# Loading q in 1 KB runs of four tokens, with rows un-permuted in the store, 64x64 state tiles, a new load order and a list-scheduled TensorE order

## The chip, the cores and the metric

The kernel runs on one core of one Trainium2 chip. The metric is the device time in microseconds of one launch. Fast runs of one kernel lie within 1.3% of each other. The profiles are single executions; their spans are about 2 us shorter than the timed runs. A "step" below is one block of 128 tokens of one batch entry (24 steps), a "chunk" is 512 tokens, that is four steps (6 chunks).

In profile lines PE is TensorE, PEld its weight loads, DVE is VectorE, ACT is ScalarE, POOL is GpSimd, SP is SyncE, which issues the loads. PEclk is the clock that TensorE was granted, in tenths of full speed; DMA is the mean busy share of the 16 DMA engines. A line number such as L335 is the line of the kernel's text that recorded the instruction; it differs between kernels.

## The reference, cut to what matters

Decaying linear attention over blocks of 64 tokens, then a feed-forward layer with a sine-squared activation:

```python
# q, k, v: (4, 8, 768, 64) float32; lam: (8,)
for b in range(nb):
    intra = einsum('bhic,bhjc->bhij', qb, kb) * Dmask        # lam ** (i - j), causal
    intra = einsum('bhij,bhjd->bhid', intra, vb)
    inter = einsum('bhid,bhde->bhie', qb * lam_pow, kv_state)
    out[:, :, sl] = intra + inter
    kv_state = lam_block * kv_state + einsum('bhsd,bhse->bhde', kb_dec, vb)
x = out.transpose(0, 2, 1, 3).reshape(3072, 512)
h = x @ w_in                                                  # 512 -> 2048
s = sin(alpha * h)
return (h + s * s / (alpha + 1e-9)) @ w_out                   # 2048 -> 512
```

## The kernel before

The kernel is a list of operations, each with an engine, an assumed duration and its dependencies. A small model orders the operations of all engines but TensorE; TensorE follows the order in which they were recorded. It works on blocks of 128 tokens: scale q and k by powers of lam, transpose them (on TensorE for steps 0 to 12, by DMA from step 13 on), S = scores of the eight heads, mask, then per step O (state times q, plus S times v) and Z (new state). Each of the eight heads has 64 columns; two heads share the 128 rows.

```python
def load_one(nme, s):                    # one DMA of 256 KB for each of k, q, v of a step
    a = src[b, :, n * BL:(n + 1) * BL, :].rearrange("h p d -> p h d")      # runs of 64 floats = 256 B
    rec_load(lambda e: e.dma_start(dst[r][:, :, :], a), [f"{nme}32.{r}"], f"{nme}{r}", 321000, ...)

# att_O: state part, then scores times v, then the new state
for jp in range(HP):                     # four 128x128 matmuls on a block-diagonal state
    e.matmul(dst[:, jp, :], Zs[(s - 1) % 2][:, jp, :], qkT[jq][:, jp, :], start=(jp == 0), stop=False, ...)
for jp in range(HP):
    for h in range(2):                   # eight matmuls of 128 rows, 64 columns
        last = e.matmul(dst[64*h:64*h+64, jp, :], v2[c][:, 2*jp+h, :], S_m[j][:, 4*h+jp, :], ...)
# ... Z: eight 128x64 matmuls, then two copies of the state out of PSUM, one for each half

# store of 128 tokens: 128 rows of 2 KB
rec("ACT", lambda e: e.dma_start(out[row0:row0 + 128, :], osb[o][:, :]), 0, ...)

# start: loads k0 q0 k1 q1 v0 k2 q2 v1 k3 q3 v2 v3; then per step s = 0..3
#   att_S(s); warm(2); att_T(s + 1); warm(1); att_O(s)      (warm: dummy matmuls)
# then chunk 0: 16 groups grp_A (x @ w_in), 16 groups grp_B (@ w_out) with attention steps 4 to 7 at
# hand-picked places; chunk 1's grp_A with steps 8 to 11; from there grp_B(c) and grp_A(c + 1) alternate
```

Of the kernel before, what the change touches and what calls it, by code (L numbers as in the profile page):

```python
# [28 lines left out]
class Program:  # L29
# [41 lines left out]
    def schedule(self, hop=0.12, rate=270e3, lag=1.7, receipt=1.0, issue=0.6, begin=0.75, depth=2):  # L71
# [15 lines left out]
        pe_at = 0  # L87
# [5 lines left out]
        def release(op):  # L93
            for u in op.users:
                left[u] -= 1
                same = u.eng == op.eng and op.slot is None
                ready_at[u] = max(ready_at[u], op.end + (0.0 if same and op.eng == "PE" else hop))
                if not left[u] and u.eng != "PE":
                    pend[u.eng].append(u)
# [5 lines left out]
        def transfer(t, i):  # L105
            _, op = (sw, hw)[i].pop(0)
            if i and len(hw) == depth - 1:
                free["SP"] = max(free["SP"], t)
            op.end = t + op.nbytes / rate + receipt
            release(op)  # L110
            return op.end - receipt

        n = len(self.ops)
        while len(order) < n:
            best = None
            for e in self.ENGINES:
                if e == "PE":
                    if pe_at >= len(pe_seq):
                        continue
                    op = pe_seq[pe_at]  # L120
                    if left[op]:
                        continue
                    cand = (max(free[e], ready_at[op]), op)
                else:
                    if not pend[e] or (e == "SP" and len(hw) >= depth):
                        continue
                    t0 = min(max(free[e], ready_at[o]) for o in pend[e])
                    op = min((o for o in pend[e] if max(free[e], ready_at[o]) <= t0 + 1e-9),
                             key=lambda o: (o.prio, o.idx))
                    cand = (t0, op)  # L130
# [8 lines left out]
            e = op.eng  # L139
            if e == "PE":  # L140
                pe_at += 1
            else:
                pend[e].remove(op)
            op.start = t
            order.append(op)
            for u in op.soft_users:
                left[u] -= 1
                ready_at[u] = max(ready_at[u], op.start)
                if not left[u] and u.eng != "PE":
                    pend[u.eng].append(u)  # L150
# [79 lines left out]
def bass_lightning_attn__then__act_snake_kernel(  # L230
# [23 lines left out]
    NQ = 3  # L254
    FIRST_DT = 13
# [4 lines left out]
    NO = 4  # L260

    es = contextlib.ExitStack()
    with es:
# [9 lines left out]
        q32 = ring("q32", RL, [128, H, D], F32)  # L273
# [3 lines left out]
        q2 = [t[:, 0, :, :] for t in qk2]  # L277
# [3 lines left out]
        S_m = ring("S_m", 2, [128, 8, 128], BF16)  # L281
        Zs = ring("Zs", 2, [128, HP, 128], BF16)
# [7 lines left out]
        mask = sb("mask", [128, 128], BF16)  # L290
# [3 lines left out]
        lam_bc = sb("lam_bc", [128, H], F32)  # L294
        E_i = sb("E_i", [128, NB, H], I32)
        E_f = sb("E_f", [128, NB, H], F32)
        lnlam = sb("lnlam", [128, H], F32)
        lnL = sb("lnL", [128, NB, H], F32)
        Lq = sb("Lq", [128, NB, H], F32)
# [26 lines left out]
        wblk, gate = [], {}  # L326
# [4 lines left out]
        def load_one(nme, s):  # L331
            src, dst = {"k": (k, k32), "q": (q, q32), "v": (v, v32)}[nme]
            b, n, r = s // NB, s % NB, s % RL
            a = src[b, :, n * BL:(n + 1) * BL, :].rearrange("h p d -> p h d")
            rec_load(lambda e: e.dma_start(dst[r][:, :, :], a), [f"{nme}32.{r}"], f"{nme}{r}", 321000,  # L335
                     [gate[s]] if s in gate else [])
# [6 lines left out]
        def consts():  # L343
            rec("ACT", lambda e: e.dma_start(lam_bc[:, :], bass.AP(lam.tensor, 0, [[0, 128], [1, H]])), 0,
                writes=["lam"], slot="lam", nbytes=4096)
            rec("ACT", lambda e: e.preload_act_table_set("natural_log_exp_and_others"), 1.3, writes=["table"])
            rec("POOL", lambda e: e.memset(zeros[:, :], 0.0), 0.5, writes=["zeros"])
            rec("POOL", lambda e: e.iota(E_i[:, :, :], [[128, NB], [0, H]], base=0, channel_multiplier=1), 0.2,
                writes=["E_i"])
            rec("DVE", lambda e: e.tensor_copy(E_f[:, :, :], E_i[:, :, :]), 0.2, reads=["E_i"], writes=["E_f"])  # L350
            rec("ACT", lambda e: e.activation(lnlam[:, :], lam_bc[:, :], ACTF.Ln), 0.3,
                reads=["lam", "table"], writes=["lnlam"])
            ln_b = bass.AP(lnlam, 0, [[H, 128], [0, NB], [1, H]])
            rec("DVE", lambda e: e.tensor_tensor(lnL[:, :, :], E_f[:, :, :], ln_b, ALU.mult), 0.2,
                reads=["E_f", "lnlam"], writes=["lnL"])
            rec("ACT", lambda e: e.activation(Lq[:, :, :], lnL[:, :, :], ACTF.Exp), 0.3,
                reads=["lnL"], writes=["Lq"])
            rec("ACT", lambda e: e.activation(Lk[:, :, :], lnL[:, :, :], ACTF.Exp, scale=-1.0), 0.3,
                reads=["lnL"], writes=["Lk"])
            rec("DVE", lambda e: e.memset(maskf[:, :], 0.0), 0.2, writes=["maskf"])  # L360
# [4 lines left out]
                out=mask[:, :], in_=maskf[:, :], pattern=[[-1, 128]], compare_op=ALU.is_gt, fill=1.0,  # L365
# [4 lines left out]
            for i in range(2):  # L370
                rec("DVE", lambda e, i=i: e.memset(Zs[i][:, :, :], 0.0), 0.3, writes=[f"Zs.{i}"])
# [15 lines left out]
        def w_block(j, soft=(), after=()):  # L387
            if j < 4:
                cs = slice(512 * j, 512 * (j + 1))
                src = moe_w_in[:, cs].rearrange("(c p) f -> p c f", p=128)  # L390
                op = rec("POOL", lambda e: e.dma_start(w1[:, :, cs], src), 0.85, writes=[f"w1.{j}"],
                    slot=f"w1_{j}", nbytes=723000, soft=soft, after=after)
            else:
                j2 = j - 4
                src = moe_w_out[512 * j2:512 * (j2 + 1), :].rearrange("(m p) d -> p m d", p=128)
                op = rec("POOL", lambda e: e.dma_start(w2[:, 4 * j2:4 * (j2 + 1), :], src), 0.85, writes=[f"w2.{j2}"],
                    slot=f"w2_{j2}", nbytes=723000, soft=soft, after=after)
            wblk.append(op)

        def prep(s, fast=False, soft=()):  # L400
            n, r, c = s % NB, s % RL, s % RC
            Lq_b = bass.AP(Lq, n * H, [[NB * H, 128], [1, H], [0, D]])
            Lk_b = bass.AP(Lk, n * H, [[NB * H, 128], [1, H], [0, D]])
            dve_k, dve_q = s == 3, fast and s != 2
            done = rec("DVE" if dve_k else "POOL", lambda e: e.tensor_tensor(k2[c], k32[r][:, :, :], Lk_b, ALU.mult),
                       0.65 if dve_k else 1.05, reads=[f"k32.{r}", "Lk"], writes=[f"k2.{c}"], soft=soft)
            rec("DVE" if dve_q else "POOL", lambda e: e.tensor_tensor(q2[c], q32[r][:, :, :], Lq_b, ALU.mult),
                0.65 if dve_q else 1.05, reads=[f"q32.{r}", "Lq"], writes=[f"q2.{c}"], soft=soft)
            if not soft:
                prep_v(s)  # L410
# [7 lines left out]
        def prep_v(s, soft=()):  # L418
            r, c = s % RL, s % RC
            rec("ACT", lambda e: e.copy(v2[c][:, :, :], v32[r][:, :, :]), 0.62,  # L420
                reads=[f"v32.{r}"], writes=[f"v2.{c}"], soft=soft)

        def att_T(s, bank=None):
# [8 lines left out]
            def pe(e):  # L432
                for jp in range(HP):
                    last = e.transpose(dst[:, jp, :], q2[c][:, 2 * jp:2 * jp + 2, :], ident[:, :])  # L434
# [3 lines left out]
            rec("PE", pe, 0.5, reads=[f"q2.{c}", f"k2.{c}", "ident"], writes=[key])  # L438
            rec("DVE", lambda e: e.tensor_copy(qkT[j][:, :, :], dst), 0.7, reads=[key], writes=[f"qkT.{j}"], prio=-1)  # L439

        def att_S(s):
            j, j2 = s % NQ, s % 2

            def pe(e):
                for jp in range(HP):
                    for h in range(2):
                        rows = slice(64 * h, 64 * h + 64)
                        last = e.matmul(A_ps[:, 4 * h + jp, :], qkT[j][rows, 4 + jp, :], qkT[j][rows, jp, :])  # L448
# [280 lines left out]
```

## Time and profile before

| | before |
|---|---|
| median of the timed runs | 225.18 us (224.98 to 225.64, 3 runs) |
| first feed-forward matmul (chunk 0, first half) | 23.04 us |
| second half of chunk 0 begins | 37.77 us |
| chunk 1 begins | 60.50 us |
| second half of chunk 1 begins | 81.48 us |
| TensorE ends / span ends | 220.20 / 222.92 us |

The milestones are start times of the first matmul of each group of feed-forward matmuls in the trace. From the page of the kernel before: busy time of the engines, then the span in 40 slices of 5.6 us (a digit is tenths), then the queue of the loads.

```profile
span 222.9 us, 3787 instructions
...
PE 209.1 (94%) x1513; PEld 102.9 (46%) x1539; DVE 119.7 (54%) x160; ACT 121.8 (55%) x216; POOL 133.9 (60%) x141
...
PE   6865999998999999999999999999999999999995
...
PEclk9999799999999999999999999999999999999999
DMA  6999999999999999999999533063031011100212
...
q1 hardware_dynamic: 86640, 21.90, 52.3%
...
PE 81%; DVE 6%; SPq 5%; DMA 3%; ACT 2%; issue 2%; POOL 0%
```

TensorE is busy nearly everywhere after the fourth slice. DMA reads 9 (90% or more) from slice 2 to slice 22, to some 120 us, and 6 or less after that. The last line, from the chain of work that ended last, puts 81% of the span on TensorE. So TensorE bounds the long second half, and loads bound the start.

The DMA issues of the same page, with count, size and median time from issue to landing:

```profile
out_dram<-osb ACTq DMA_DIRECT2D x23, 256.0 KB, 2.7
...
k_0<-in_k_dram SPq DMA_DIRECT2D x4, 256.0 KB, 5.1
q_0<-in_q_dram SPq DMA_DIRECT2D x4, 256.0 KB, 4.8
...
qkT<-qk_3 SPq DMA_TRANSPOSE x3, 3.2
```

### The profile page before, as it was taken

The page shows a single profiled execution, that of the slowest core. Times are in us where ns is not written, and L with a number is a line of the kernel's source. Part 1 is how long each engine was busy: PE and PEld are TensorE (multiplying, and loading weights), DVE is VectorE, ACT ScalarE, POOL GpSimd, SP SyncE. Part 2 cuts the span into 40 slices and gives each one's busy share as a digit, 9 for nine tenths or more (in the row PEclk, how much of TensorE's full clock was granted, in tenths as well). Part 3 has the DMA queues.
Part 4 walks back from the last instruction along what each step waited for, and adds up shares of the span by engine and source line. Part 5 has one row for each costly group of instructions (what it writes and reads, how often), then busy time and mean ns, then how long its engine had stood idle before and what let it go on. Part 6 is the DMA issues. An engine that isn't in the chain of part 4 may idle for free.

```text
span 222.9 us, 3787 instructions
## 1 busy us (share of the span) xinstructions
PE 209.1 (94%) x1513; PEld 102.9 (46%) x1539; DVE 119.7 (54%) x160; ACT 121.8 (55%) x216; POOL 133.9 (60%) x141
## 2 busy tenths in 40 slices
PE   6865999998999999999999999999999999999995
PEld 2443344454555444445445444445445444444454
DVE  2674189736868994645545454553553535544300
ACT  3354688131498976575575556566556435544220
POOL 3464378661389998668768867867845553355000
PEclk9999799999999999999999999999999999999999
DMA  6999999999999999999999533063031011100212
GB/s 133 219 216 201 195 196 220 162 229 229 268 284 221 222 201 236 215 244 180 245 221 201 141 94 94 1 96 96 19 79 47 0 50 47 47 37 10 79 65 94
DMA packets 94513, 32.50 MB, mean 146 GB/s; under 512 B 87184, under 2 KB 91552, under 8 KB 94496
## 3 DMA queue, kind: packets, MB, share of 16 engines
q1 hardware_dynamic: 86640, 21.90, 52.3%
q0 software_dynamic: 4224, 4.19, 11.4%
q10 hardware_dynamic: 3632, 6.17, 7.6%
q8 instruction: 12, 0.20, 0.4%
q14 instruction: 5, 0.04, 0.1%
HBM read 27.28 MB, written 6.29 MB: 151 GB/s over the span
## 4 chain that ended last, share of the span: by engine, by line
PE 81%; DVE 6%; SPq 5%; DMA 3%; ACT 2%; issue 2%; POOL 0%
PE m_ps L509 34%; PE m_ps L537 34%; SPq L335 5%; PE A_ps L473 3%; PE A_ps L448 3%; DMA v_3<-in_v_dram 3%; DVE gT L527 2%; PE A_ps L469 2%; PE m_ps L562 2%; DVE S_m L453 1%; PE A_ps L434 1%; PE Z_ps L488 1%; PE A_ps L436 1%; DVE u_3 L525 1%; DVE qkT L439 1%
## 5 line engine op out<-in xcount | busy, mean ns | idle before, releaser
L509 PE MATMUL m_ps<-xT,w 128*128 128x512 bf16 x366 | 92.5, 382 | 2.3 <-issue 1.7
L537 PE MATMUL m_ps<-w,gT 128*128 128x512 bf16 x362 | 90.6, 379 | 0.6 <-issue 0.3
L537 PEld LDWEIGHTS m_ps<-w,gT 128*128 128x128 bf16 x368 | 34.9, 98 | 42.2 <-ACT osb L549 1.3
L509 PEld LDWEIGHTS m_ps<-xT,w 128*128 128x128 bf16 x384 | 35.1, 98 | 41.3 <-issue 1.5
L453 DVE TENSOR_TENSOR S_m<-A_ps,mask 128x1024 bf16<-128x1024 f32 x24 | 29.4, 1223 | 9.7 <-PE A_ps L448 9.7
L525 POOL TENSOR_TENSOR u_0<-t_0 128x512 bf16<-128x512 bf16 x16 | 16.6, 1038 | 13.9 <-ACT t_0 L513 13.9
L527 DVE SCALAR_TENSOR_TENSOR gT<-u_3,r_sb,m_ps 128x512 bf16<-128x512 bf16 x16 | 11.9, 744 | 15.0 <-POOL u_3 L525 14.9
L482 ACT CAST xT<-A_ps 128x512 bf16<-128x512 f32 x20 | 11.7, 586 | 15.1 <-PE A_ps L473 15.0
L525 POOL TENSOR_TENSOR u_2<-t_2 128x512 bf16<-128x512 bf16 x15 | 15.6, 1037 | 7.3 <-ACT t_2 L513 7.3
L525 POOL TENSOR_TENSOR u_4<-t_4 128x512 bf16<-128x512 bf16 x15 | 15.6, 1039 | 7.0 <-ACT t_4 L513 7.0
L527 DVE SCALAR_TENSOR_TENSOR gT<-u_5,r_sb,m_ps 128x512 bf16<-128x512 bf16 x16 | 11.9, 746 | 14.1 <-POOL u_5 L525 14.1
L527 DVE SCALAR_TENSOR_TENSOR gT<-u_1,r_sb,m_ps 128x512 bf16<-128x512 bf16 x16 | 11.9, 744 | 14.0 <-POOL u_1 L525 14.0
L527 DVE SCALAR_TENSOR_TENSOR gT<-u_0,r_sb,m_ps 128x512 bf16<-128x512 bf16 x16 | 11.9, 743 | 11.5 <-POOL u_0 L525 11.5
L549 ACT COPY osb<-m_ps 128x512 f32<-128x512 f32 x19 | 11.1, 585 | 11.7 <-PE m_ps L537 11.7
L525 POOL TENSOR_TENSOR u_5<-t_5 128x512 bf16<-128x512 bf16 x12 | 12.5, 1039 | 7.9 <-ACT t_5 L513 7.8
L513 ACT ACTIVATE t_0<-m_ps,alpha_sb 128x512 bf16<-128x512 f32 x16 | 11.0, 685 | 10.8 <-PE m_ps L509 10.8
L513 ACT ACTIVATE t_2<-m_ps,alpha_sb 128x512 bf16<-128x512 f32 x16 | 11.0, 687 | 10.7 <-PE m_ps L509 10.5
L525 POOL TENSOR_TENSOR u_3<-t_3 128x512 bf16<-128x512 bf16 x12 | 12.5, 1038 | 7.3 <-ACT t_3 L513 7.2
L513 ACT ACTIVATE t_4<-m_ps,alpha_sb 128x512 bf16<-128x512 f32 x16 | 11.0, 687 | 10.7 <-PE m_ps L509 10.7
L525 POOL TENSOR_TENSOR u_1<-t_1 128x512 bf16<-128x512 bf16 x12 | 12.4, 1037 | 7.2 <-ACT t_1 L513 7.2
L496 ACT CAST Zs<-Z_ps 64x256 bf16<-64x256 f32 x40 | 14.6, 366 | 1.6 <-DVE qkT L439 1.0
L513 ACT ACTIVATE t_3<-m_ps,alpha_sb 128x512 bf16<-128x512 f32 x16 | 11.0, 687 | 8.0 <-PE m_ps L509 8.0
(190 smaller groups left out, 238.0 us busy)
## 6 DMA issues: line engine op xcount, KB each, us to landing
out_dram<-osb ACTq DMA_DIRECT2D x23, 256.0 KB, 2.7
w<-in_moe_w_in_dram POOLq DMA_DIRECT2D x4, 512.0 KB, 11.5
w<-in_moe_w_out_dram POOLq DMA_DIRECT2D x4, 512.0 KB, 12.8
k_0<-in_k_dram SPq DMA_DIRECT2D x4, 256.0 KB, 5.1
q_0<-in_q_dram SPq DMA_DIRECT2D x4, 256.0 KB, 4.8
k_1<-in_k_dram SPq DMA_DIRECT2D x4, 256.0 KB, 5.2
q_1<-in_q_dram SPq DMA_DIRECT2D x4, 256.0 KB, 5.6
v_0<-in_v_dram SPq DMA_DIRECT2D x4, 256.0 KB, 4.9
```

Source lines behind the costliest of these rows:

```text
L335: rec_load(lambda e: e.dma_start(dst[r][:, :, :], a), [f"{nme}32.{r}"], f"{nme}{r}", 321000, [gate[s]] if s in gate else [])
L448: last = e.matmul(A_ps[:, 4 * h + jp, :], qkT[j][rows, 4 + jp, :], qkT[j][rows, jp, :])
L453: rec("DVE", lambda e: e.tensor_tensor(S_m[j2][:, :, :], A_ps[:, :, :], mask_b, ALU.mult), 1.25, reads=["S0", "S1", "mask"], writes=[f"S_m ...
L473: last = e.matmul(dst[64 * h:64 * h + 64, jp, :], v2[c][:, 2 * jp + h, :], S_m[j][:, 4 * h + jp, :], start=(not has_state and jp == 0), st ...
L482: rec("ACT", lambda e: e.copy(xT[x][:, :, col:col + 128], dst), 0.6, reads=[key], writes=[f"x.{x}.{s % 4}"], prio=-1)
L496: rec("ACT", lambda e, rows=rows, cols=cols: e.copy(Zs[j][rows, :, cols], Z_ps[rows, :, :]), 0.4, reads=["Z"], writes=[f"Zs.{j}"])
L509: last = e.matmul(m_ps[i][:, :], w1[:, kc, 128 * m:128 * (m + 1)], xT[x][:, kc, :], start=(kc == 0), stop=(kc == NKC - 1))
L513: rec("ACT", lambda e: e.activation(t16[tt][:, :], m_ps[i][:, :], ACTF.Sin, scale=alpha_sb[:, m:m + 1]), 0.65, reads=[f"m.{i}", "alpha"], ...
L525: return e.tensor_tensor(u16[tt][:, :], t16[tt][:, :], t16[tt][:, :], ALU.mult)
L527: rec("DVE", lambda e: e.scalar_tensor_tensor(out=gT[g][:, m, :], in0=u16[tt][:, :], scalar=r_sb[:, m:m + 1], in1=m_ps[i][:, :], op0=ALU.m ...
L537: last = e.matmul(m_ps[bank][:, :], gT[g][:, m, 128 * s4:128 * (s4 + 1)], w2[:, m, :], start=(m == 0), stop=(m == NM - 1))
L549: rec("ACT", lambda e: e.copy(osb[o][:, :], m_ps[bank][:, :]), 0.6, reads=[f"m.{bank}"], writes=[f"o.{o}"])
```

## The change

Its intent: q in runs of 256 B costs the DMA engines more per byte than longer runs (in the trace a packet of 256 B takes 18 ns and one of 1 KB 46 ns), and loads bound the start. If a partition holds four neighbouring tokens of one head, a run is 1 KB. The tokens of a block then come out in another order (all with token mod 4 = 0 first, and so on), which the mask takes into account and the store undoes. Beside that, the state is kept as 64x64 tiles (one copy out of PSUM instead of two), k and q are loaded first and v last, the first w_in block is halved, and TensorE's order comes from list scheduling: of the next 40 recorded operations the model takes the one that is ready, with 0.2 us of slack for those recorded earlier.

The diff, cut to its core:

```diff
 # load
+            if nme == "q":
+                for h in range(2):
+                    a = src[b, h::2, n * BL:(n + 1) * BL, :].rearrange("g (p t) d -> g p (t d)", t=4)
+                    rec_load(lambda e, h=h, a=a: e.dma_start(
+                        q32[r][:, h, :, :].rearrange("p t d -> p (t d)"), a), [f"q32.{r}.{h}"], f"q{r}{h}", 112000)
 # store
-                rec("ACT", lambda e: e.dma_start(out[row0:row0 + 128, :], osb[o][:, :]), 0,
+                dst = out[row0:row0 + 128, :].rearrange("(p t) d -> t p d", t=4)
+                rec("ACT", lambda e: e.dma_start(dst, osb[o][:, :]), 0,
 # q columns of head pair jp, for S and for the state matmuls
+            return qkT[j][rows, 0:4, 32 * jp:32 * jp + 32]
 # state: 64x64 tiles, Z recorded before O
-                        e.matmul(dst[:, jp, :], Zs[(s - 1) % 2][:, jp, :], qkT[jq][:, jp, :], ...
+                        for h in range(2):
+                            rows = slice(64 * h, 64 * h + 64)
+                            e.matmul(dst[rows, jp, :]..., Zs[(s - 1) % 2][rows, jp, :], q_cols(jq, rows, jp), ...
 # TensorE order
-                    op = pe_seq[pe_at]
+                    ready = [o for o in ready if pe_rank[o] < pe_at + window]
+                op = min((o for o in ready if max(free[e], ready_at[o]) <= t0 + (slack if e == "PE" else 0) + 1e-9), ...
 # start
-        for what in ("k0", "q0", "k1", "q1", "v0", "k2", "q2", "v1", "k3", "q3", "v2", "v3"):
+        for what in ("k0", "q0", "k1", "q1", "k2", "q2", "k3", "q3", "v0", "v1", "v2", "v3"):
 # ... start: prep, transposes and scores of steps 0 to 3 first, then their output matmuls;
 # steps 4 to 7 recorded before grp_B of chunk 0, all their scalings released by chunk 0's last grp_A;
 # DMA transposes from step 12 on; more buffers for qkT and S_m (cut)
```

## The prediction

> **What bounds the kernel now.** The page gives TensorE 94% busy and 81% of the chain that ended last. Three phases:
>
> 1. Start-up, 0 to 23.0 us (timeline: first feed-forward matmul at 23.04 us), bound by the load queue: twelve q, k, v loads leave one per 1.18 us, the last (v of step 3) landing at 19.10 us. Then 3.9 us of chain: v copy, xT copy, two state copies (0.76 us), state and score matmuls at a granted clock of 0.66, xT copy.
> 2. First chunk, 23 to 60.5 us. DMA share is about 1.2; TensorE has 1.6 us of visible gaps between 40 and 58 us, the largest, 0.95 us, for q of step 7, landed at 53.27 us.
> 3. Steady state, 60.5 to 220 us, bound by TensorE alone. 512-column matmuls start every 216 ns. Each change between full and half-array shapes adds about 93 ns of spacing (149 instead of 56 ns between the last state matmul and the first S_m matmul).[...] A step costs about 0.43 us for S and 0.79 us for state, S_m and Z matmuls.
>
> **What the change does.**
>
> - q loads: 1024 packets of 256 B (18 ns median each) become 256 of 1 KB; 1 KB packets of the last stores took 46 ns. Estimate over 16 engines: 1.15 us becomes 0.74, so 0.4 us per step: 1.6 us by step 3, 3.3 us by step 7.[...]
> - v last, a first w1 block of half size, v copies spread over POOL, DVE and ACT, one state copy for two: v of step 3 lands near 17 us, the chain after it shrinks to 2 to 2.5 us. First feed-forward matmul: 19.3 us (18.3 to 20.5), a gain of 3.7 us, all critical.
> - First chunk: list scheduling and lighter loads remove 1 to 2 us of gaps. The second chunk's first group starts near 55.3 us instead of 60.5.
> - 64x64 state matmuls: four at 56 ns become four pairs at about 56 ns, no gain by themselves. Z first and the 64x64 shape add up to two shape changes per step with state: +0.19 us at worst[...]. I take +0.08 us over 13 such steps: +1 us, critical in the steady state.
> - One transposed step less on TensorE: -0.45 us.
> - Score, weight, tail and store work: unchanged (store packets stay 2 KB).
>
> Sum: -5.2 + 1.0 - 0.4 = -4.6 us.
>
> **Predicted time: 220.6 us, 217.5 to 223.8 in 8 of 10. Faster by over 2%: 0.50; within 2%: 0.47; slower by over 2%: 0.03.**
>
> **What would show it right or wrong.** Timeline: first feed-forward matmul near 19.3 us. DMA packets: 25,000 fewer of 256 B, 6,000 more of 1 KB, near 46 ns. Waits: 40 to 58 us loses the wait for q. Steady state: last 64x64 state matmul to first S_m matmul near 149 ns[...]; second chunk's start to the end 162.4 us before, 162 to 164 after.
>
> **What would make it wrong.** TensorE sits too idle before 19 us and starts at a low clock; w1 blocks land later than the earlier matmuls need them, giving the start-up gain back as waits; shape changes cost the full 0.19 us; the modelled TensorE order mispredicts landings and stalls; or, on the good side, the list schedule closes more gaps.

Four passages are cut where marked. -5.2 us at the start and in the first chunk (60.5 to 55.3), +1.0 for the changes of shape and -0.4 for one transposed step less give the -4.6 us.

## More of the kernel before

The longest waits of TensorE before (total us, times, longest):

```profile
PE m_ps L469 <- ACT Zs L496: 1.8, 1, 1.8
PE m_ps L579 <- POOL ident L361: 1.8, 1, 1.8
...
PE A_ps L434 <- DVE qk_2 L407: 1.0, 1, 1.0
```

No wait of the whole kernel is longer than 1.8 us.

## The result, and the profile after

The changed kernel takes 284.85 us (284.2 to 285.32, 4 runs) against 225.22 us before (with a fourth run); the ratio of the fast runs is 1.2643 (95% interval 1.2611 to 1.2675). Here and below a ratio is the mean time of one kernel's fast runs over that of the kernel before in the same rounds, so it isn't quite the ratio of the medians quoted. The change is 60 us slower where I had predicted 4.6 us faster.

From the page after:

```profile
span 282.4 us, 3953 instructions
...
PE 225.5 (80%) x1587; PEld 106.8 (38%) x1613; DVE 121.6 (43%) x158; ACT 117.7 (42%) x198; POOL 137.9 (49%) x147
...
PE   7447895899768687099939938967999999999990
...
PEclk9995699799997999689988997995999999999997
DMA  3469998797435568787586579695123111111122
...
q1 hardware_dynamic: 69060, 22.16, 39.5%
...
PE 56%; DMA 21%; SPq 11%; DVE 5%; issue 2%; ACT 1%; POOL 1%; POOLq 0%
```

TensorE's busy time grew from 209 to 225 us, but its share fell from 94% to 80%, and on the chain that ended last DMA went from 3% to 21%, the SP queue from 5% to 11%. The DMA row reads 5 to 8 through most of slices 5 to 28, where before it read 9: loads still hold the kernel back, and for longer, but with fewer DMA engines busy: the mean share of these slices is 0.75, where it was 1.15 in slices 2 to 22 before (the share can read above 1).

The milestones of the two traces (start of the first feed-forward matmul of each group), in us:

| | before | after | stretch up to this row longer by |
|---|---|---|---|
| v of step 3 landed | 19.10 | 27.18 | |
| chunk 0 first half begins | 23.04 | 30.53 | 7.5 (start) |
| chunk 0 second half begins | 37.77 | 50.77 | 5.5 |
| chunk 1 begins | 60.50 | 75.95 | 2.5 |
| chunk 1 second half begins | 81.48 | 105.36 | 8.4 |
| TensorE ends | 220.20 | 275.75 | 31.7 |
| span ends | 222.92 | 282.39 | 3.9 (tail) |

More than half of the loss lies behind the point from which I had called the kernel bound by TensorE alone. TensorE waits there for transposes that go by DMA, 22.3 us in all. The longest waits of TensorE after (total us, times, longest):

```profile
PE A_ps L480 <- DMA qkT<-qk_2: 13.4, 2, 7.8
PE A_ps L480 <- DMA qkT<-qk_0: 4.6, 1, 4.6
PE m_ps L577 <- DVE gT L567: 4.6, 1, 4.6
```

The DMA issues of the kernel after:

```profile
out_dram<-osb ACTq DMA_DIRECT2D x23, 256.0 KB
...
k_0<-in_k_dram SPq DMA_DIRECT2D x4, 256.0 KB, 7.6
q_0<-in_q_dram SPq DMA_DIRECT2D x8, 128.0 KB
...
qkT<-qk_2 SPq DMA_TRANSPOSE x3, 8.1
```

Two things stand out. The same k load that took 5.1 us from issue to landing takes 7.6 us, and transposes that took 3.2 to 3.8 us before take 4.8 to 8.1 us. And the two kinds of DMA whose shape was changed, the loads of q and the stores, have lost their landing time altogether. The SP queue shows how long each issue of a load held it at the start. Before (start us, us, engine, line, operation):

```profile
5.71 1.14 SPq L335 DMA_DIRECT2D k_2<-in_k_dram  x1
6.90 1.14 SPq L335 DMA_DIRECT2D q_2<-in_q_dram  x1
8.09 1.13 SPq L335 DMA_DIRECT2D v_1<-in_v_dram  x1
```

After:

```profile
8.31 1.05 SPq L345 DMA_DIRECT2D k_2<-in_k_dram  x1
9.41 2.60 SPq L341 DMA_DIRECT2D q_2<-in_q_dram  x2
12.05 1.33 SPq L345 DMA_DIRECT2D k_3<-in_k_dram  x1
13.43 2.76 SPq L341 DMA_DIRECT2D q_3<-in_q_dram  x2
```

One tile of q holds the queue for 2.6 us, where it held it for 1.14 us. I had estimated 0.74 us.

The packets, counted by size on the load queue, say why. They add up to the page's totals (86,640 and 69,060):

```
load queue          256 B     1 KB    4 B
before             84,992      128   1,520
after              61,440    6,272   1,348
```

The packets of 1 KB have a median of 46 ns and those of 256 B 18 ns, both as predicted. The last column is the key. The number of 4-byte packets is a fixed one for each DMA, and the counts agree exactly: before, 72 loads x 16 + 11 transposes x 32 + 1 half store x 16 = 1,520. After, 48 loads of k and v x 16 + 12 transposes x 32 + 48 loads of q x **4** + 1 half store x **4** = 1,348. The source of a q load, `"g (p t) d -> g p (t d)"`, has the four head pairs as its slowest dimension, where the loads with 16 have 128 tokens. The store, `"(p t) d -> t p d"`, has the 4 of the token order as its slowest dimension; on its queue the 4-byte packets went from 416 (26 DMAs x 16) to 132 (25 x 4 + 2 x 16).

The same number shows in how many packets are under way at a time, counted from their start times and durations in the two traces. Of the time that any is under way, the 1 KB packets of the load queue after are most often four at a time (41%; 7 at most), and so are the 2 KB packets of the stores (57%; 7 at most). Before, the 2 KB packets of the stores are most often 16 at a time (22%; 20 at most). So I read the number of 4-byte packets of a load or a store as the number of DMA engines that work on it, and say "on 4 engines" for it; the traces don't name the engine of a packet. In this case's profiles every issue group on fewer than 16 engines in this sense lacks its landing time. That is what the missing numbers meant.

An estimate from these durations fits: a k tile is 1024 packets of 18 ns on 16 engines, 1.15 us; a q tile is 2 DMAs of 128 packets of 46 ns on 4 engines, 2 x 32 x 46 ns = 2.94 us. Together 4.1 us for each pair of k and q; in the trace k of steps 1, 2 and 3 lands at 10.32, 14.25 and 18.13 us, 3.9 us apart. Before, one load landed every 1.18 us.

### The profile page after: what moved, and what is told of

Read it like the earlier page. It is cut to its first block, busy times and chain, and to the rows that moved or that the text cites. A ratio compares the mean times of both kernels' runs of the same rounds, so it can differ in the third digit from the quotient of the medians.

```text
span 282.4 us, 3953 instructions
## 1 busy us (share of the span) xinstructions
PE 225.5 (80%) x1587; PEld 106.8 (38%) x1613; DVE 121.6 (43%) x158; ACT 117.7 (42%) x198; POOL 137.9 (49%) x147
## 3 DMA queue, kind: packets, MB, share of 16 engines
q1 hardware_dynamic: 69060, 22.16, 39.5%
## 4 chain that ended last, share of the span: by engine, by line
PE 56%; DMA 21%; SPq 11%; DVE 5%; issue 2%; ACT 1%; POOL 1%; POOLq 0%
PE m_ps L577 24%; PE m_ps L549 24%; SPq L341 8%; DMA qkT<-qk_2 6%; SPq L345 4%; DMA qkT<-qk_0 3%; DMA w<-in_moe_w_out_dram 3%; DMA qkT<-qk_4 3%; DMA q_5<-in_q_dram 2%; PE A_ps L480 2%; DMA v_3<-in_v_dram 2%; DMA v_1<-in_v_dram 2%; DVE u_1 L565 2%; PE A_ps L526 1%; PE A_ps L522 1%
## 5 line engine op out<-in xcount | busy, mean ns | idle before, releaser
L549 PE MATMUL m_ps<-xT,w 128*128 128x512 bf16 x365 | 98.2, 399 | 3.8 <-issue 2.3
L577 PE MATMUL m_ps<-w,gT 128*128 128x512 bf16 x362 | 94.9, 391 | 5.2 <-DVE gT L567 4.6
L577 PEld LDWEIGHTS m_ps<-w,gT 128*128 128x128 bf16 x368 | 35.7, 101 | 50.8 <-issue 6.5
L549 PEld LDWEIGHTS m_ps<-xT,w 128*128 128x128 bf16 x384 | 36.0, 101 | 45.8 <-issue 6.8
L480 PE MATMUL A_ps<-qkT 64*128 64x128 bf16 x192 | 10.9, 241 | 24.6 <-DMA qkT<-qk_2 13.4
L567 DVE SCALAR_TENSOR_TENSOR gT<-u_3,r_sb,m_ps 128x512 bf16<-128x512 bf16 x16 | 11.9, 745 | 19.4 <-POOL u_3 L565 19.3
L480 PEld LDWEIGHTS A_ps<-qkT 64*128 64x128 bf16 x192 | 6.3, 102 | 35.1 <-issue 19.9
L567 DVE SCALAR_TENSOR_TENSOR gT<-u_0,r_sb,m_ps 128x512 bf16<-128x512 bf16 x16 | 11.9, 744 | 15.7 <-POOL u_0 L565 15.7
L589 ACT COPY osb<-m_ps 128x512 f32<-128x512 f32 x21 | 12.3, 585 | 15.1 <-PE m_ps L577 15.0
L567 DVE SCALAR_TENSOR_TENSOR gT<-u_5,r_sb,m_ps 128x512 bf16<-128x512 bf16 x16 | 11.9, 746 | 15.3 <-POOL u_5 L565 15.3
L567 DVE SCALAR_TENSOR_TENSOR gT<-u_1,r_sb,m_ps 128x512 bf16<-128x512 bf16 x16 | 11.9, 744 | 13.8 <-POOL u_1 L565 13.8
L553 ACT ACTIVATE t_5<-m_ps,alpha_sb 128x512 bf16<-128x512 f32 x16 | 11.0, 686 | 16.1 <-PE m_ps L549 16.1
L553 ACT ACTIVATE t_1<-m_ps,alpha_sb 128x512 bf16<-128x512 f32 x16 | 11.0, 686 | 15.5 <-PE m_ps L549 15.5
L567 DVE SCALAR_TENSOR_TENSOR gT<-u_2,r_sb,m_ps 128x512 bf16<-128x512 bf16 x16 | 11.9, 742 | 12.0 <-POOL u_2 L565 12.0
L553 ACT ACTIVATE t_2<-m_ps,alpha_sb 128x512 bf16<-128x512 f32 x16 | 11.0, 687 | 13.8 <-PE m_ps L549 13.7
```

The lines of the kernel that those rows point to most:

```text
L480: last = e.matmul(A_ps[:, 4 * h + jp, :].rearrange("p (t i) -> p t i", t=4), qkT[j][rows, 4 + jp, :], q_cols(j, rows, jp))
L549: last = e.matmul(m_ps[i][:, :], w1[:, kc, 128 * m:128 * (m + 1)], xT[x][:, kc, :], start=(kc == 0), stop=(kc == NKC - 1))
L553: rec("ACT", lambda e: e.activation(t16[tt][:, :], m_ps[i][:, :], ACTF.Sin, scale=alpha_sb[:, m:m + 1]), 0.65, reads=[f"m.{i}", "alpha"], ...
L567: rec("DVE", lambda e: e.scalar_tensor_tensor(out=gT[g][:, m, :], in0=u16[tt][:, :], scalar=r_sb[:, m:m + 1], in1=m_ps[i][:, :], op0=ALU.m ...
L577: last = e.matmul(m_ps[bank][:, :], gT[g][:, m, 128 * s4:128 * (s4 + 1)], w2[:, m, :], start=(m == 0), stop=(m == NM - 1))
L589: rec("ACT", lambda e: e.copy(osb[o][:, :], m_ps[bank][:, :]), 0.6, reads=[f"m.{bank}"], writes=[f"o.{o}"])
```

## The experiments

Theory A: most of the loss comes from q loads and stores on 4 of the 16 DMA engines. Rivals: the 1 KB packets themselves are slow (A'), or the new TensorE order and the new start stall on mispredicted landings whatever the engines do (A''). More theories came up on the way. "Before" in a ratio is the kernel before, run in the same rounds on the same chip. All runs gave correct results. Fast runs are compared with fast runs: one run of `lockfree` (242.09 us), and one of the kernel before beside `q16` (227.20 us), fell in the slow state.

### q on 16 engines

`q16` is the kernel after with q loaded in four DMAs, one for each head pair, so that the slowest dimension is the 32 runs of a head. Packets, their sizes and all else stay.

```diff
-for h in range(2):
-    a = src[b, h::2, tokens].rearrange("g (p t) d -> g p (t d)", t=4)
+for g in range(4):
+    a = src[b, 2*g:2*g+2, tokens].rearrange("h (p t) d -> p h (t d)", t=4)     # -> rows 32g to 32g+31
```

> The changed kernel with one edit: each q tile is loaded by four DMAs, one per pair of heads, whose slowest dimension is 32 instead of 4; same 1 KB packets, same data, same stores. Theory A (the q loads ran on 4 of the 16 DMA engines, because the slowest dimension of their source is 4): a k and q pair takes about 1.9 us of the load queue instead of 3.9, the first feed-forward matmul comes at 19 to 21 us instead of 30.5, the waits for transposed q and k vanish, time 220 to 227 us (the stores still have 4 as slowest dimension, which leaves the tail some 3.5 us longer than before). Rival B (the TensorE order from list scheduling stalls in order because its model is wrong): the order is nearly the same, so time stays above 260 us.[...]

A third rival, C, the 64x64 state tiles, expected over 270 us.

Measured: 244.69 us, ratio 1.0871 (1.0817 to 1.0925). The load queue and the q loads of its page:

```profile
q1 hardware_dynamic: 70404, 22.16, 52.5%
...
q<-in_q_dram SPq DMA_DIRECT2D x96, 64.0 KB, 4.8
```

The landing time is back; the 4-byte packets are 2,692 (768 + 96 x 16 + 384 + 4), the packets of 1 KB still 6,272. v of step 3 lands at 18.71 us instead of 27.18, and TensorE's waits for transposes fall from 22 us to 0.3 us. So 40.2 of the 59.6 us are gone with the packets unchanged: A' is out, and A'' can own at most the rest. But the time misses my 220 to 227 us by some 18 us, so theory A alone is not the whole loss. The k, q pair still costs 2.5 us: its five DMAs take about 0.5 us each to issue.

### q on 2 engines

`q2` goes the other way: the same four DMAs for each tile, each with two head pairs as the slowest dimension. It has the DMA count of `q16`, so it also separates the engines from the number of DMAs.

```diff
+for h in range(2):
+    for gp in range(2):
+        a = src[b, 4*gp+h : 4*gp+h+3 : 2, tokens].rearrange("g (p t) d -> g p (t d)", t=4)
```

> The changed kernel with the q loads cut the other way: four DMAs per tile, each with a slowest dimension of 2. Same number of q DMAs as q16, same packets. Theory A: q of one step now takes 128 packets x 46 ns = 5.9 us on 2 engines, a k and q pair about 7 us; time 340 to 420 us[...]. Rivals B and C, or a cost of the number of DMAs: within 5% of 285 us.

Measured: 333.14 us, ratio 1.4804 (1.4704 to 1.4903; two runs), just below the 340 to 420 us that I expected. v of step 3 lands at 37.72 us. The 4-byte packets are 1,348 again (96 x 2 = 192 = 48 x 4). With 2, 4 and 16 engines for the same bytes the kernel takes 333, 285 and 245 us.

### The kernel before with q on 4 engines

`before_k4` changes nothing in the kernel before but the cut of the q load into 124 and 4 partitions. Packets stay 256 B. That a DMA of 124 rows runs on 4 engines, like one of 4 rows, was my assumption; the 4-byte packets of the result agree with it.

```diff
-rec_load(... dst[r][:, :, :], a ...)
+for p0, p1 in ((0, 124), (124, 128)):
+    rec_load(... dst[r][p0:p1, :, :], a[p0:p1] ...)          # q only
```

> The kernel before, unchanged but for the q loads: each is cut into 124 and 4 partitions[...]; packets stay 256 B, order and everything else stay. Theory A (number of engines): q of one step takes 256 packets x 18 ns = 4.6 us on 4 engines, a k, q, v step about 6.9 us instead of 3.5, the first feed-forward matmul comes at 34 to 40 us, time 250 to 285 us. Rival (the change is slow through its order or its shapes, not through the engines): within 3% of 225 us.

Measured: 254.89 us, ratio 1.1339 (1.1278 to 1.1401). The first feed-forward matmul moved from 23.04 to 44.83 us, later than my 34 to 40: v of step 3 landed only at 40.92 us. The w_in blocks were issued at 22.2 us, just before the last v loads at 23.4 us, and may have held them up; no run tests that. Its 4-byte packets are 1,328 = 48 x 16 + 48 x 4 + 11 x 32 + 16. So 4 engines for q cost the otherwise unchanged kernel 30 us, in the old order and with the old packets. Theory A is shown from both sides.

### Stores

The store has the same flaw. `q16_stA` is `q16` with each store cut into four DMAs, one for each residue of the token, on 16 engines each (their landing time is back, 2.4 us). `q16_stB` is `q16` with a plain store; the rows are put in order by the copy that writes xT.

```diff
 # q16_stA
+for t in range(4):
+    dma_start(out[row0:row0+128, :].rearrange("(p t) d -> t p d", t=4)[t], osb[o][32*t:32*t+32, :])
 # q16_stB
+copy(xT[x][:, :, cols].rearrange("p a (i t) -> p a t i", t=4), dst.rearrange("p a (t i) -> p a t i", t=4))
+dma_start(out[row0:row0+128, :], osb[o][:, :])
```

> q16, and each store cut into four DMAs of 32 rows, so that no DMA has a slowest dimension under 16. Theory A: the tail from the last matmul to the end goes from about 6.5 us back to about 3 us; time 217 to 223 us. Rival B: over 260 us.

> q16, with the rows un-permuted in the xT copy out of PSUM instead of in the store, so that the stores are those of the kernel before (one DMA of 128 rows). Theory A: as q16_stA within 1%, with the xT copy's duration near 0.59 us if its strided write is free; if the strided write costs, the copy shows it.

Measured: `q16_stA` 244.88 us (1.0876), no different from `q16`, where I expected 217 to 223; `q16_stB` 241.53 us (1.0733), 3.2 us better than `q16` and 1.4% below `q16_stA`, where I expected 1% at most. The tail from the last matmul to the end of the span is 6.54 us in `q16`, 3.64 in `q16_stA`, 2.82 in `q16_stB`, and 2.72 before, so stores on 4 engines do cost 3 to 4 us at the end. `q16_stA` gives that back elsewhere (below). `q16_stB` pays with an xT copy of 1.30 us instead of 0.59 on ScalarE, which is not all hidden: its first feed-forward matmul comes at 27.05 us, in `q16` at 25.88.

### A VectorE instruction held by GpSimd

What remains of the loss? `q16` has one wait of TensorE that sticks out:

```profile
PE m_ps L578 <- DVE gT L568: 4.9, 1, 4.9
```

VectorE in `q16` at that time (start us, us):

```profile
37.70 1.39 DVE L568 SCALAR_TENSOR_TENSOR gT<-u,r_sb,m_ps 128x512 bf16<-128x512 bf16 x2
39.02 5.98 DVE L433 TENSOR_TENSOR qk<-q,Lq 128x512 bf16<-128x512 f32 x1
44.93 0.73 DVE L568 SCALAR_TENSOR_TENSOR gT<-u,r_sb,m_ps 128x512 bf16<-128x512 bf16 x1
```

GpSimd in `q16` at that time:

```profile
39.42 2.05 POOL L566 TENSOR_TENSOR u<-t 128x512 bf16<-128x512 bf16 x2
41.42 1.04 POOL L431 TENSOR_TENSOR qk<-k,Lk 128x512 bf16<-128x512 f32 x1
42.42 1.03 POOL L566 TENSOR_TENSOR u<-t 128x512 bf16<-128x512 bf16 x1
43.42 1.03 POOL L431 TENSOR_TENSOR qk<-k,Lk 128x512 bf16<-128x512 f32 x1
```

A scaling of q that takes 0.69 us elsewhere took 5.98 us and ended at 45.00 us, 0.55 us after GpSimd's run without gaps (44.45 us). The kernel after shows the same at 45.23 us, with a square that took 4.82 us and ended 0.29 us after GpSimd's run. Theory B: both operands of that VectorE instruction lie in SBUF, and it can't proceed while GpSimd works through instructions without a gap. That the two inputs in SBUF matter was my assumption. Rival: this scaling is slow by itself, for its operand or its place.

`lock4` moves the q scaling of steps 4 and 7 to GpSimd; nothing else changes against `q16_stA`.

```diff
-prep_next(4, soft=[op], eng_q="DVE")
+prep_next(4, soft=[op], eng_q="POOL")      # and the same for step 7
```

> q16_stA with the q scaling of steps 4 and 7 moved from VectorE to GpSimd. Theory L (in q16 the VectorE scaling of q of step 4 takes 5.9 us instead of 0.7 because GpSimd runs back to back beside it[...]): no VectorE instruction over 1.5 us at that place, the feed-forward wait of 4.8 us for gT vanishes, time 239 to 241 us against 244.9. Rival (the scaling waits for its data, q of step 4): the same instruction waits on GpSimd, time within 1 us of 244.9.

Measured: 248.17 us (1.1044), 3.3 us slower than `q16_stA`, where I expected 239 to 241 us. The hold did not go away; it moved to another instruction with two SBUF inputs, a square of the activation, as VectorE of `lock4` shows:

```profile
39.51 6.83 DVE L566 TENSOR_TENSOR u<-t 128x512 bf16<-128x512 bf16 x1 [0.74 <-ACT t L554]
```

It stood beside seven GpSimd instructions in a row, from 39.02 to 46.05 us. The rival falls: it isn't the scaling. `lockfree` therefore also moves the two squares of chunk 0 that VectorE did at that time to ScalarE.

```diff
-if (c == 0 and m in (3, 8, 13)) or ...        # square on VectorE
+if (c == 0 and m == 3) or ...
-elif (c == 0 and m in (5, 10, 15)) or ...     # square on ScalarE
+elif (c == 0 and m in (5, 8, 10, 13, 15)) or ...
```

> lock4, and the squares of groups 8 and 13 of the first chunk moved from VectorE to ScalarE, so that VectorE has no instruction with two SBUF inputs while GpSimd runs back to back. lock4 moved the long instruction from the q scaling (5.9 us) to the square (6.8 us) beside the same GpSimd run. Theory L (any VectorE instruction with two SBUF inputs is held while GpSimd runs without a gap): no VectorE instruction over 1.5 us, first chunk's first to second half 15 to 17.5 us instead of 20.6, time 239 to 242 us against 244.9 of q16_stA. Rival (it is the load on VectorE that is late, whatever the instruction): another VectorE instruction becomes long, time unchanged within 1 us.

Measured: 239.56 us over four runs, 238.66 over the three fast ones (1.0626, 1.0553 to 1.0699). By the fast runs that is 6.2 us better than `q16_stA` (5.6 by the ratios) and 9.5 better than `lock4`. The first half of chunk 0 takes 14.82 us, as in the kernel before (14.73), instead of 20.62. Theory B is shown for these two instructions: with none of two SBUF inputs on VectorE there, none is held (from 36 to 44 us its instructions take 0.70 to 0.75 us each). What holds them is not shown; the runs show the hold and when it ends. It is also not a rule that such an instruction is held. In the kernel before, GpSimd works from 35.51 to 42.56 us with no gap but a DMA issue of 0.81 us, and these three instructions, two of VectorE and one of GpSimd, go through beside each other:

```profile
37.25 0.58 DVE L525 TENSOR_TENSOR u_1<-t_1 128x512 bf16<-128x512 bf16 x1
37.51 1.22 POOL L405 TENSOR_TENSOR qk_4<-k_4,Lk 128x512 bf16<-128x512 f32 x1
39.07 1.21 DVE L407 TENSOR_TENSOR qk_4<-q_4,Lq 128x512 bf16<-128x512 f32 x1
```

I took the cause in the change to be that all scalings of steps 4 to 7 are released by one matmul group, which gives GpSimd more work in a row. No run shows that: `start_old` below keeps that release, and its longest VectorE instruction of two SBUF inputs there takes 1.21 us. What decides whether one is held stays open.

### The start order

In `q16_stA` v of step 3 has landed at 18.66 us, 0.4 us before the kernel before has it, yet the first feed-forward matmul comes at 25.75 us, 2.7 us later. ScalarE of `q16_stA`, with the wait before an instruction in brackets:

```profile
22.30 0.58 ACT L444 CAST xT<-m_ps 128x512 bf16<-128x512 f32 x1 [0.76 <-PE m_ps L527]
22.79 0.62 ACT L444 CAST v<-v 128x512 bf16<-128x512 f32 x1
24.70 0.58 ACT L444 CAST xT<-m_ps 128x512 bf16<-128x512 f32 x1 [1.30 <-PE m_ps L527]
```

v of step 3 was copied 4 us after it had landed, behind the xT copy of step 2. With v last, the output matmuls of all four steps come in a row at the end; their longest wait, 1.20 us, ends with this copy of v. TensorE works at a granted clock near 0.5 from 16 to 28 us (before: 1.00 in the first 4 us of these). Its groups of eight score or output matmuls take 0.60 to 0.64 us there instead of 0.40. Theory C: the new load order and start cost time by themselves. Rival: they gain, and the rest of the loss is elsewhere. `start_old` is `q16_stA` with the load order and the start of the kernel before; `lf_start` is `lockfree` with them.

```diff
-for what in ("k0", "q0", "k1", "q1", "k2", "q2", "k3", "q3", "v0", "v1", "v2", "v3"):
+for what in ("k0", "q0", "k1", "q1", "v0", "k2", "q2", "v1", "k3", "q3", "v2", "v3"):
+# per step 0 to 3: att_S(s); warm(2); att_T(s + 1); warm(1); att_O(s); whole first w_in block;
+# the mask of step 2 waits for the q scaling of step 3, as before
```

> q16_stA with the start of the kernel before: v of step 0 after q of step 1 and so on, each step's output matmuls right after its scores, first w1 block whole, mask of step 2 held until q of step 3 is scaled. Theory S (with v last, four output steps stand in a row behind the transposes of step 3 and run at half clock, so that the first feed-forward matmul comes 7 us after v of step 3 instead of 4): first feed-forward matmul at 21.5 to 23.5 us instead of 25.75, time 241 to 243. Rival (it is the loads): unchanged at 25 to 26 us.

> lockfree and start_old together. If the two effects are separate they add: about 6 to 8 us below q16_stA, 236 to 239 us, still above the kernel before by list scheduling and the 64x64 tiles.

Measured: `start_old` 239.2 us (1.0645), 5.7 us better than `q16_stA` and better than my 241 to 243; `lf_start` 235.81 us (1.0481, 1.0442 to 1.052), 2.9 us better than the fast runs of `lockfree` (3.3 by the ratios). First feed-forward matmul: 23.52 and 23.70 us instead of 25.75 and 26.32. The two repairs don't add up, since `start_old` also shortened the longest held VectorE instruction, to 1.21 us. So v last, with the start that goes with it, loses some 3 us; the theory holds, though the runs don't split its parts (order of loads, order of copies, clock). The clock alone doesn't separate them: `lf_start` too has 0.50 from 20 to 28 us.

### The other parts, each alone on the kernel before

`lf_start` is still 10.6 us above the kernel before. Its remaining parts were put into the kernel before one at a time: `before_64` has the 64x64 state tiles with one copy; `before_q` has q in 1 KB runs in the four DMAs of `q16` with mask, decay table, the four-part store of `q16_stA` and the load queue modelled in bytes; `before_st4` has only a store in four parts of 32 rows, nothing permuted; `before_ls` has only the new scheduling function (list scheduling of TensorE, and the load queue modelled in bytes); `before_q64` is `before_q` with the 64x64 tiles.

```diff
 # before_64: four 128x128 state matmuls become eight 64x64, no zeroed off-diagonal
+e.matmul(dst[rows, jp, :], Zs[(s - 1) % 2][rows, jp, :], qkT[jq][rows, jp, :], ...)     # rows of head h
+rec("ACT", lambda e: e.copy(Zs[j][:, :, :], Z_ps[:, :, :]), ...)                         # one copy
 # before_st4
-dma_start(out[row0:row0+128, :], osb[o][:, :])
+for t in range(4):
+    dma_start(out[row0+32*t:row0+32*t+32, :], osb[o][32*t:32*t+32, :])
 # before_ls: schedule() replaced by the changed one, nothing else
```

> The kernel before with the 64x64 state tiles alone (eight 64x64 matmuls and one state copy for four matmuls and two copies). My prediction took +1 us (0 to +3.7). [...]about 0.09 us more between the state matmuls and what follows, +1.5 to +3 us, time 226 to 229. If the saved state copies matter: 223 to 225.

What is cut before "about 0.09 us more" is its condition: that each change of tile shape costs time.

> The kernel before with one part alone: q in 1 KB runs on 16 engines (four DMAs per tile), mask and decay table to match, stores cut in four DMAs that un-permute rows; order, state tiles and start as before. My prediction's 0.4 us per q tile is worth at most the 0.5 us that four issues leave of it: start shortened by 0 to 1 us, gaps of the first chunk by 0 to 1, a tail about 0.9 us longer (q16_stA's was 3.64 us against 2.72): time 223.5 to 226. Rival (1 KB runs are worth 3 us by step 7): 221 to 223.

> The kernel before with each store cut into four DMAs of 32 whole rows and nothing permuted. before_q lost 5.3 us. If the four store issues on ScalarE's queue cost it: 227 to 229 us here, with steady state 1 us longer and a tail of 3.3 us. If not, 225 to 226 and the loss is in the q loads.

> The kernel before with list scheduling of the TensorE order alone (window 40, slack 0.2 us), everything else as before. If list scheduling closes gaps as my prediction had it: 223 to 224.5 us. If its model misjudges arrivals so that TensorE stalls in order: 226 to 231. I expect within 1.5% of before.

> before_q with the 64x64 state tiles. If the parts add (5.3 and 1.7 us): 231 to 233 us, and what remains up to lf_start's 235.8 is list scheduling and the order of the first chunk, about 4 us.

Measured:

| | median us | before | ratio (95%) | costs, us |
|---|---|---|---|---|
| before_64 | 226.39 | 224.61 | 1.0074 (1.0033 to 1.0115) | 1.7 |
| before_q | 230.19 | 224.89 | 1.0243 (1.0203 to 1.0283) | 5.5 |
| before_st4 | 229.42 | 224.40 | 1.0236 (1.0173 to 1.0300) | 5.3 |
| before_ls | 227.73 | 224.40 | 1.0150 (1.0096 to 1.0204) | 3.4 |
| before_q64 | 232.31 | 224.40 | 1.0352 (1.0302 to 1.0402) | 7.9 |

(The last column is the ratio less 1, times the median of the kernel before. At the threshold of 2% `before_st4` and `before_ls` are unclear and `before_64` counts as the same, but all intervals lie above 1.) `before_q` misses my 223.5 to 226 us. Stores in four parts, list scheduling and 64x64 tiles sum to 10.4 us, near the 10.6 us that were left of `lf_start`. `lf_start` also has Z ahead of the state matmuls, DMA transposes from step 12 on and the new record order of chunk 0, which no run tests alone, so part of this agreement is luck. The cost of `before_q` is that of its stores alone, within 0.2 us, so the q loads in 1 KB runs on 16 engines gained nothing and lost nothing measurable (the two intervals leave room for some 1.7 us either way). `before_q64` is 2.4 us above `before_q`, somewhat more than the 1.7 us of the tiles alone.

Where the four-part stores cost: each issue takes about 0.5 us of ScalarE's own time, and ScalarE also makes xT, the state copies and the activations. ScalarE of `before_st4`, and after it the same place in the kernel before:

```profile
58.83 4.47 ACTq L553 DMA_DIRECT2D out_dram<-osb  x9
63.35 0.37 ACT L496 CAST Zs<-Z_ps 64x256 bf16<-64x256 f32 x1 [3.94 <-DVE S_m L453]
```

```profile
59.95 0.94 ACTq L552 DMA_DIRECT2D out_dram<-osb  x2
```

Nine issues in a row hold ScalarE for 4.47 us, where two held it for 0.94 us, and the state copy comes only after them (the profile puts its wait down to VectorE, whose instruction had ended 0.4 us earlier). TensorE then waits 1.9 us for the copy of v behind it, which is the largest part of the 5.3 us that I can point to. So the split traded engines for issue time on a busy queue, which may be why `q16_stA` was no better than `q16`.

The 64x64 tiles: in a steady stretch the spacing from a feed-forward matmul to the first state matmul is 309 ns in `before_64` (median) and 216 ns in the kernel before, 93 ns more; state to scores times v stays at 146 (149) ns. In `q16_stA`, where Z also stands ahead of the state matmuls, feed-forward to Z is 309, and Z to state 126 ns where pairs within the Z group are 28 ns apart. So both extra changes of shape are there, about 0.19 us for each step with state, and the stretch from the second half of chunk 1 to TensorE's end is 1.2 us longer in `before_64` (139.94 against 138.72) and 2.8 us longer in `q16_stA` (141.56).

### Two DMAs for q on 16 engines

Can the four DMAs for each q tile be had as two? `qp_nat` is the kernel after with partition = 4 x quad of tokens + head pair, so the slowest dimension is the 32 quads. Columns of q are then read in token order with a stride, mask and store are plain. `before_qp_t` is `before_q` with the same two DMAs, but its columns are read with token mod 4 outermost.

```diff
-a = src[b, h::2, tokens].rearrange("g (p t) d -> g p (t d)", t=4)
+a = src[b, h::2, tokens].rearrange("g (p t) d -> p g (t d)", t=4)
 # q columns of head pair jp
+qp_nat:       qkT[j][rows, 0:4, jp:jp+125:4].rearrange("r t i -> r i t")     # steps of 256 bytes
+before_qp_t:  qkT[j][rows, 0:4, jp:jp+125:4]                                 # steps of 8 bytes
```

> The changed kernel with partition = 4 x quad + head pair for q, so that a q load has 32 as slowest dimension in two DMAs and not four, and TensorE reads the q columns in token order (steps of 128 and 4 elements), so that no row needs un-permuting and the stores are those of before. Theory A: a k and q pair takes about 1.9 us of the load queue (q16 took 2.5, bound by five issues of 0.5 us), time 236 to 241 us if TensorE reads strided columns at full speed. If strided reads are slower, the S matmuls start further apart than 56 ns a pair, and time goes up by as much.

> before_q with partition = 4 x quad + head pair, so that q takes two DMAs on 16 engines, and TensorE reads the 32 columns of a head pair 4 elements (8 bytes) apart. qp_nat read at steps of 256 bytes and its S matmuls started 220 ns apart a pair, against 56. If 8-byte steps run at full rate: S pairs 56 ns apart, load queue of a k and q pair 1.9 us, time 224 to 228 us. If any step slows the read: 110 to 220 ns a pair, +0.2 to +0.7 us in S and as much in the state matmuls per step, time 234 to 250.

Measured: 262.65 us (1.168) and 238.76 us (1.062). `qp_nat` misses the 236 to 241 us for reads at full speed by over 20 us; `before_qp_t` falls in the 234 to 250 us that I had put down for slow reads. The loads did what I wanted: v of step 3 lands at 16.69 and 17.07 us, the only runs near the 17 us of the prediction, with landing times on q and on the store. The price is on TensorE. The spacing of pairs of score matmuls (medians, start to start) is:

```
q columns read as        run           pair to pair
4 x 32 contiguous        q16_stA        56 ns
steps of 8 bytes         before_qp_t   115 ns
steps of 256 bytes       qp_nat        223 ns
```

Steps of 8 bytes, which are 4 bf16, doubled the spacing, and steps of 256 bytes made it four times as long. With up to 12 or 16 such matmuls for each of 24 steps, the additional time is on TensorE, where the kernel is bound.

### An earlier chunk 0, and a hybrid

`before_warm` is the kernel before with eight dummy matmuls ahead of the output matmuls of step 3, to keep the granted clock up. It tests what a gain at the start is worth at all.

```diff
+if s == 3:
+    warm(8)
 att_O(s, bank=s % 2)
```

> The kernel before with eight more dummy matmuls in front of the output matmuls of step 3, where TensorE idles for 2.2 us and its granted clock falls to 0.66. If the clock is held: the row of steps 3 output matmuls and the first feed-forward matmuls run at full clock, first chunk's first half 14.0 us instead of 14.7, first feed-forward matmul 0 to 0.5 us earlier, time 0.5 to 1.3 us below before. If not, within 0.3 us of it. Both theories of the change's loss leave this open; it is tried as a version that may beat both kernels.

Measured: 225.19 us, ratio 0.9994 (0.9956 to 1.0031). The windows of the kernel before and of `before_warm` (stretch, length, then busy us and count of PE, PEld, DVE, ACT, POOL, granted clock, DMA share, GB/s):

```profile
20.00:30.00 10.00, 8.77 (x49) 4.17 (x51) 3.09 (x6) 6.40 (x13) 3.93 (x4) 0.83 1.22 196
```

```profile
20.00:30.00 10.00, 9.32 (x60) 4.35 (x59) 4.11 (x7) 7.27 (x14) 4.07 (x4) 1.00 1.21 195
```

The clock is 1.00 instead of 0.83, and the first half of chunk 0 takes 13.95 us instead of 14.73. The second half then takes 25.11 us instead of 22.73: all of it is given back before chunk 1 begins, at 62.11 us against 60.50 (the profiled run was the slowest of its six, so part of this is spread). The loads fit this: q of steps 5, 6 and 7 lands at 41.0, 47.3 and 53.2 us here and at 40.8, 47.5 and 53.3 us before, so what TensorE gains ahead of them it can lose waiting for them. This is read from two traces, and the interval of the time still allows a gain of 1.0 us; no run shortened the start by the 3.7 us of my prediction.

`hyb_warm` was the last try for a kernel that beats both: `before_warm` with q in 1 KB runs on 16 engines, and the stores as single DMAs on 4 engines (no extra issues on ScalarE) but for the last whole tile and the two halves.

> before_warm with the parts of before_q (q in 1 KB runs on 16 engines), but each store in one DMA on 4 engines as in the change, except the last tile's, cut in four over two queues. before_st4 put before_q's loss of 5.3 us into the four store issues on ScalarE's queue: then this is within 1.5 us of before_warm. If it is 3 us or more slower, q's four loads cost too.

Measured: 241.44 us (1.0699), a miss: I expected it within 1.5 us of `before_warm`, and it is 16 us slower. TensorE's longest waits in it:

```profile
PE A_ps L482 <- DMA qkT<-qk: 4.5, 1, 4.5
PE A_ps L468 <- POOL qk L441: 4.3, 2, 3.4
```

The scaling that it waits for on GpSimd waits 4.71 us for k, and transposes wait as well. `before_q` has the same q loads and stores in four parts and is 10 us faster (1.0243), and the dummy matmuls alone cost nothing (0.9994), so the single stores on 4 engines are what costs here. After the four stores issued from 56 to 62 us, k of step 10 lands at 74.58 us, in `before_q` at 66.21. That is in line with stores on 4 engines standing in the way of loads, but I have not shown it packet by packet, and in `q16` against `q16_stA` the same choice of store made no difference. No run beat the kernel before.

### Summary of the way from 284.85 to 225.18 us

| step | run | median us | gain |
|---|---|---|---|
| kernel after | after | 284.85 | |
| q on 16 engines | q16 | 244.69 | 40.2 |
| store in four parts on 16 engines | q16_stA | 244.88 | -0.2 |
| no VectorE instruction with two SBUF inputs beside GpSimd's run | lockfree (fast runs) | 238.66 | 6.2 |
| load order and start as before | lf_start | 235.81 | 2.9 |
| stores whole and plain | (before_st4) | | 5.3 |
| TensorE in recorded order | (before_ls) | | 3.4 |
| 128x128 state tiles | (before_64) | | 1.7 |

The first five rows come from runs whose kernel before had medians of 224.89 to 225.25 us; by the ratios the gains of `lockfree` and `lf_start` are 5.6 and 3.3 us. The last three are differences measured on the kernel before; that they close the gap to 0.2 us is a sum, not a run, and part of the agreement is luck, as said above.

## Why the prediction was wrong

- The step that failed is "Estimate over 16 engines: 1.15 us becomes 0.74, so 0.4 us per step". Packet counts (25,000 fewer, 6,000 more; found 23,552, as one more transpose by DMA adds 1,024, and 6,144) and 46 ns were right. "Over 16 engines" was not: the diff's own access pattern has 4 as its slowest dimension, so a tile took 2.94 us by the same arithmetic, 1.8 us more per step instead of 0.4 less. This alone is 40.2 of the 59.6 us (`q16`). I had not asked on how many engines the new pattern would run.
- "Steady state, bound by TensorE alone" held for the kernel before, not for the kernel after: its loads of later steps and its DMA transposes share the queue with the slow q loads and slipped into the steady state, which became 31.7 us longer from the second half of chunk 1 on. With q on 16 engines (`q16`) the same stretch is only 7.6 us longer (146.3 us against 138.72). I had carried the bound of one stage over to a kernel whose loads no longer finish ahead of it.
- "v of step 3 lands near 17 us": reached only with q in two DMAs on 16 engines (16.69 us in `qp_nat`, 17.07 in `before_qp_t`); in the kernel after it was 27.18. "First feed-forward matmul: 19.3 us": never below 22.04 us in any run. The chain behind the last v did not shrink from 3.9 us to 2 to 2.5; with v last it was 3.4 us in the kernel after, where v itself is late, and 7.1 us in `q16_stA`.
- "A gain of 3.7 us, all critical": doubtful. `before_warm` gained 0.8 us in chunk 0's first half and had no measurable gain at the end (0.9994). Up to chunk 1 the loads of steps 5 to 7 set the pace in both traces, and the DMA row of the page before, 9 to 120 us, should have made me ask. The gain of 3.7 us itself was reached in no run.
- "List scheduling and lighter loads remove 1 to 2 us of gaps": wrong in sign. List scheduling alone costs 3.4 us (`before_ls`), and in place of the gaps came a larger wait, behind a VectorE instruction held beside GpSimd (4.82 us in the kernel after; without it 6 us less, `lockfree`).
- "I take +0.08 us over 13 such steps: +1 us": the sign was right, the size was off. Both changes of shape occur, some 0.19 us for each step with state, my "worst" case; alone in the kernel before the tiles cost 1.7 us.
- "Score, weight, tail and store work: unchanged (store packets stay 2 KB)": wrong for stores. The packets stay, but run on 4 engines; the tail grew from 2.72 to 6.64 us, and cutting the store to get 16 engines back costs 5.3 us of issues.
- Of what I had listed as able to make it wrong, a low clock at the start (0.50) and shape changes at their full cost did occur, and the modelled order lost 3.4 us alone, but these are the small terms. The large one was not on the list.

## What to carry to other kernels

Before you predict a DMA's time from its packets, read the slowest dimension of both sides: here the DMAs whose slowest dimension is 4 ran on 4 engines, one q tile taking the load queue for 2.6 us instead of 1.14, however good its runs were. In the profile a busy load queue beside a DMA row that is not full (5 to 8 tenths here), or an issue group without a landing time, was the sign of it. Cutting such a DMA to regain engines cost about 0.5 us of issue for each piece here (nine on ScalarE in 4.47 us, four of q in 1.99 us), and on ScalarE's busy queue 5.3 us of the kernel's time (`before_st4`). Check, too, whether the stage after the one that you shorten is bound by something else, and look in the profile after for a VectorE instruction with two SBUF inputs that takes several times its usual length beside GpSimd (5.98 us instead of 0.69 here).
